# A recurrent attention kernel: one left residual load on ScalarE's queue, main rows stored straight from SBUF, and four steps of the attention one unit later on TensorE

## The chip, the core and the metric

The kernel runs on one core of a Trainium2 chip. The metric is the device time of one execution in microseconds; lower is better. Engines are called by what they do: TensorE (PE in the profile, its weight loads PEld), VectorE (DVE), ScalarE (ACT), GpSimd (POOL) and SyncE (SP, which here only issues DMAs).

## What is computed

The input x (2048 x 1024) is layer-normalised. Two branches read the result and are added to x: a dense GELU block B, and an attention A with 32 heads of 128 that runs over 64 segments of 32 rows, one after the other. Each segment is joined with 8 memory rows, and the first 8 rows of its output are the memory rows of the next segment. That makes A a recurrence:

```python
for s in range(n_seg):                      # 64 segments of 32 rows
    xs = x[:, s * seg_len:(s + 1) * seg_len, :]
    h = concatenate([mem, xs], axis=1)      # 8 + 32 rows
    q = einsum('btd,dhe->bhte', h, Wq)      # k and v alike, from Wk and Wv
    scores = einsum('bhqe,bhke->bhqk', q, k) * scale
    scores = where(mask, scores, -1e9)
    o = einsum('bhqk,bhke->bhqe', softmax(scores), v)
    o = einsum('bhte,hed->btd', o, Wo)
    mem = o[:, :M, :]
    outs.append(o[:, M:, :])
# output: x + outs + gelu(xn @ w1 + b1) @ w2 + b2, xn = layernorm(x)
```

## The kernel before

**Stages.** The layer norm and the dense block come first (lines 292 to 613, about the first 420 us); they leave the transposed rows in DRAM as `hr_d` and `hrL_d` and the residual x + B as `R_n`, which is copied from there into the second halves of `hr_d` and `hrL_d` (columns 256 to 511). Then the loop over the 64 segments runs (`for s in range(NSEG)`). Segment s has `g, i4 = divmod(s, 4)`.

**Main rows and left rows.** Only 24 of a segment's 32 rows (`NX`) must go through the recurrence with the memory rows. The other 8, the left rows, of four segments are put together into groups of 32 and carried through the same weights at fixed places: `left_k`, `left_q`, `left_v` and `left_o` say which passes of a segment take left rows along. With `i4 = 1` the output pass takes them (`left_o`), with `i4 = 0` V's first half, with `i4 = 3` (where groups follow) V's second half.

**Weights.** The 64 units of 128 x 2048 bf16 (512 KB) are K, Q and V in two halves of 8 units and O in 16. 46 units lie in SBUF for good. The other 18 are brought anew for each segment: two are copied by VectorE from PSUM (`kept`, line 241), 16 come by DMA from DRAM copies (`Wc_K`, `Wc_Q`, `Wc_V`, `Wc_O`) through six slots. SyncE issues these loads in the order of use, each when `unit_done` (the unit was multiplied) frees a slot.

**The order within a segment** is written by hand; each engine works its instructions in program order. The passes are K0, Q0, K1, Q1, V0, V1 (`half_pass`) and the output pass over the 16 units of O. A `half_pass` takes a dictionary `at`: what is called after which unit. The attention of a half u is made in three steps between the weight products: `scores(u)` (products into the PSUM bank `mixed`, an exponential on ScalarE into `pr_all`, two minima on VectorE as mask), `sums(u)` (sums over the keys, logarithm and two exponentials on ScalarE, two products on VectorE) and `values(u)` (products with V into accumulator banks, copies by ScalarE and VectorE into `d_oL` for u = 0 and `b_oL` for u = 1). The O units 0 to 7 read `d_oL`, 8 to 15 `b_oL`. There are three accumulator banks.

**Residuals and stores.** After the output pass ScalarE copies the memory part of the accumulator (line 1005), TensorE turns it into the next rows (`put_mem`), and VectorE adds the residual (line 1020): `st["res"]` in `hr_home` for main rows, at `left_o` first `st["resL"]`, which lies in `pr_all` (part of `half_home`), for the second half of the columns. `resL` is loaded on GpSimd's queue after the output pass's second unit (line 1000). The main rows of a segment are loaded by `load_x_rows`, through ScalarE's queue for s < 5 and GpSimd's after that. In the first segments GpSimd's queue also carries the last residual copies (`small`, line 455).

Stores of finished rows go through GpSimd: at `left_o` by way of `outL_d`, with i4 = 0 and 3 as four DMAs straight from SBUF (line 1058), and with i4 = 2 by way of `outM_d`: one store to DRAM on GpSimd's queue (line 1052), and in the next segment's output pass, after its third unit, one copy from DRAM to the output on SyncE's queue (`rows_of_main`, line 1055).

Of the kernel before, what the change touches and what calls it, by code (L numbers as in the profile page):

```python
# [10 lines left out]
BF16 = mybir.dt.bfloat16  # L11
# [6 lines left out]
P = 128  # L18
# [19 lines left out]
NX = 24  # L38
NL = SEG - NX
GRP = 4  # L40
NGRP = NSEG // GRP
# [45 lines left out]
def kernel(  # L87
# [16 lines left out]
    nc = tc.nc  # L104
# [3 lines left out]
    out_flat = out.rearrange("b s d -> (b s) d")  # L108
# [10 lines left out]
    dram = ctx.enter_context(tc.tile_pool(name="dram", bufs=1, space=bass.MemoryType.DRAM))  # L119
# [3 lines left out]
    hrL_d = dram.tile([NGRP + 1, P, 512], BF16, name="hrL_d")  # L123
    R_n = dram.tile([S, DM], BF16, name="R_n")
    outL_d = dram.tile([NGRP, 2 * SEG, DM], BF16, name="outL_d")
    outM_d = dram.tile([NGRP, P, 256], BF16, name="outM_d")


    place = nc.lookup_mloc("DynamicDMAScratchLoc")
# [36 lines left out]
    for j in range(4):  # L166
# [11 lines left out]
        out=m, in_=m, pattern=[[1, NX]], compare_op=ALU.is_ge, fill=0.0, base=0, channel_multiplier=-1,  # L178
    )
    for half in range(2):  # L180
        m = mask_left[0:SEG, :, 8 - 8 * half:16 - 8 * half]
        nc.gpsimd.affine_select(
            out=m, in_=m, pattern=[[-8, GRP], [0, 8]], compare_op=ALU.is_ge, fill=0.0, base=0, channel_multiplier=1,
        )
        nc.gpsimd.affine_select(
            out=m, in_=m, pattern=[[8, GRP], [1 if half else 0, 8]], compare_op=ALU.is_ge, fill=0.0,
# [110 lines left out]
    with tc.tile_pool(name="ma", bufs=2) as ma, tc.tile_pool(name="mps", bufs=6, space=PSUM) as mps:  # L297
# [35 lines left out]
        for j in range(4):  # L333
            nc.sync.dma_start(
                out=o_sb[32 * j + NX:32 * j + 32, 0:8, :],
                in_=mem0[:, 256 * j:256 * j + 256].rearrange("m (h e) -> m h e", h=8),
# [4 lines left out]
        for i in range(14):  # L341
            t = slab(f"w2_{i}")[:, :].rearrange("p (c d) -> p c d", d=DM)
# [146 lines left out]
        for tg in range(4):  # L489
# [14 lines left out]
            for fb in range(FC):  # L504
                ps = mps.tile([P, 512], F32, name="ps")
                for kt in range(KT):
# [9 lines left out]
                    out=xb[:, :], in_=ps[:, :], func=ACT.Identity, bias=b1col[:, fb:fb + 1], scale=1.0  # L516
# [4 lines left out]
                    out=u[:, :], in0=u[:, :], scalar1=0.044715, scalar2=1.0, op0=ALU.mult, op1=ALU.add  # L521
# [94 lines left out]
    with tc.tile_pool(name="late", bufs=1) as late, \  # L616
# [65 lines left out]
        for s in range(NSEG):  # L682
            g, i4 = divmod(s, GRP)
# [10 lines left out]
            left_v = [i4 == 0, first or (i4 == 3 and more)]  # L694
            left_o = i4 == 1 or final
            og, slot = divmod(s + 2, GRP)
# [103 lines left out]
            def scores(u, meanwhile=None):  # L800

                kT, qL_ends = st["kT", u], ends(q_home)
                sA = mixed[:, 0:160].rearrange("p (c q) -> p c q", q=40)
                sB = mixed[:, 160:224].rearrange("p (c q) -> p c q", q=16)
                for c in range(4):
                    for j in range(4):
                        q = slice(32 * j, 32 * j + 32)
                        nc.tensor.matmul(  # L808
                            sA[q, c, :], lhsT=kT[:, 4 * c + j, :], rhs=q_home[:, 4 * c + j, :],
                            start=(c == 0), stop=True, skip_group_check=True, tile_position=(0, 32 * j),  # L810
                        )
                    for j in range(4):
                        q = slice(32 * j, 32 * j + 32)
                        nc.tensor.matmul(  # L814
                            sB[q, c, :].rearrange("p (a b) -> p a b", b=NL), lhsT=kL[u][:, 4 * c + j, :],
                            rhs=qL_ends[:, 4 * c + j, :, :],
                            start=False, stop=True, skip_group_check=True, tile_position=(0, 32 * j),
                        )
                pr = pr_all[:, 0:224]
                nc.scalar.activation(out=pr, in_=mixed[:, 0:224], func=ACT.Exp, scale=INV_SQRT_DH)  # L820
                prA = pr[:, 0:160].rearrange("p (c q) -> p c q", q=40)
                prB = pr[:, 160:224].rearrange("p (c q) -> p c q", q=16)
                if meanwhile is not None:
                    meanwhile()
                for p, m in ((prA[:, :, NL:SEG], mask_order), (prB, mask_left[:, i4, :])):
                    n = m.shape[-1]
                    nc.vector.tensor_tensor(out=p, in0=p, in1=m[:, None, :].to_broadcast([P, 4, n]), op=ALU.min)
                st["pr", u] = prA, prB
# [38 lines left out]
            def values(u, rs):  # L867

                V, (pdA, pdB) = st["V", u], st["pd", u]
                av = {r: new_acc() for r in rs}  # L870
                oV = {r: av[r][:, 0:320].rearrange("p (c b q) -> p c b q", c=4, b=2) for r in rs}
                for c in range(4):
                    for r in rs:
                        q = slice(64 * r, 64 * r + 64)
                        nc.tensor.matmul(  # L875
                            oV[r][:, c, :, :], lhsT=V[q, c * P:(c + 1) * P], rhs=pdA[q, c, :, :],
                            start=(c == 0), stop=False, skip_group_check=True, tile_position=(64 * r, 0),
                        )
                    for r in rs:
                        q = slice(64 * r, 64 * r + 64)  # L880
                        nc.tensor.matmul(
                            oV[r].rearrange("p c b (e q) -> p c b e q", q=NL)[:, c, :, ::4, :],
                            lhsT=VL[u][q, c * P:(c + 1) * P], rhs=pdB[q, c, :, :, :],
                            start=False, stop=True, skip_group_check=True, tile_position=(64 * r, 0),
                        )
                for r in rs:
                    cp = nc.vector.tensor_copy if r else nc.scalar.copy
                    out = outs[u][:, 8 * r:8 * r + 8, NL * slot:NL * slot + 40]
                    cp(out=out.rearrange("p (b c) q -> p c b q", b=2), in_=oV[r])
                    let_go(av[r])  # L890
# [66 lines left out]
            if i4 == 0 and more and not first:  # L957
                load_left_rows(g + 1, nc.scalar)
            at = {0: [lambda: scores(1)], 4: [lambda: sums(1)]}
            if left_v[1]:  # L960
                at.update({1: [lambda: values(0, (0,))], 3: [lambda: values(0, (1,))]})
            else:
                at[1] = [lambda: values(0, (0, 1))]
# [18 lines left out]
            if left_v[1]:  # L982
                at = {4: [lambda: values(1, (0,))], 6: [lambda: values(1, (1,))]}
            else:
                at = {5: [lambda: values(1, (0, 1))]}
            if left_v[1] and not first:
                at[9] = [lambda: left_values(1, psV1L)]
            at.setdefault(0, []).append(load_res)
            if i4 == 3:
                at.setdefault(2, []).append(rows_of_main)  # L990
            psX = new_acc()
            for n, unit in enumerate(O_UNITS):
                t = unit_tile(unit)
                o_product(unit, t, psX)
                unit_done(unit)
                for fn in at.get(n, ()):
                    fn()
                if n == 1 and left_o:
                    st["resL"] = pr_all
                    nc.gpsimd.dma_start(out=st["resL"][:, :], in_=hrL_d[og, :, 256:512])  # L1000
            nw = 2 if left_o else 1
            if not final:
                o_sb = nat_home
# [27 lines left out]
            if final:  # L1031
                engines = [nc.sync, nc.scalar, nc.gpsimd]
                n = 0
                for w, r in enumerate(tiles):
                    for b in range(2):
                        cs = slice(256 * (2 * b + w), 256 * (2 * b + w) + 256)
                        pieces = [(rows, slice(64 * b + m0, 64 * b + m0 + NX))]
                        for sl, row in left_rows:
                            p0 = 64 * b + NL * sl
                            pieces.append((slice(row, row + NL), slice(p0, p0 + NL)))  # L1040
                        for o, i in pieces:
                            engines[n % 3].dma_start(out=out_flat[o, cs], in_=r[i, :])
                            n += 1
            elif left_o:
                pairs = [(out_flat[rows, :], outL_d[og, m0:m0 + NX, :])]
                pairs += [
                    (out_flat[row:row + NL, :], outL_d[og, NL * sl:NL * sl + NL, :]) for sl, row in left_rows
                ]
                for o, r in pairs:
                    small.append(lambda o=o, r=r: nc.gpsimd.dma_start(out=o, in_=r))  # L1050
            elif i4 == 2:
                nc.gpsimd.dma_start(out=outM_d[g, :, :], in_=res[:, :])
                o = out_flat[rows, :].rearrange("t (j c) -> j t c", j=4)
                r = outM_d[g, :, :].rearrange("(j t) c -> j t c", j=4)[:, 0:NX, :]
                rows_of_main = lambda o=o, r=r: nc.sync.dma_start(out=o, in_=r)
            else:
                for j in range(4):
                    nc.gpsimd.dma_start(out=out_flat[rows, 256 * j:256 * j + 256], in_=res[32 * j:32 * j + NX, :])
# [37 lines left out]
```

## Time and profile before

| | |
|---|---|
| median of 4 runs | 1881.68 us (1877.14 to 1893.29) |
| the profiled execution | 1885.86 us, of it 1884.2 us span |
| granted TensorE clock, mean | 0.993 |
| TensorE matmul busy | 1726.1 us (92%) |
| VectorE, ScalarE, GpSimd busy | 902.5, 650.9, 233.7 us |
| weight and other loads on SyncE's queue (q1) | 590.16 MB, 82.9% of 16 DMA engines |
| GpSimd's queue (q0), ScalarE's queue (q10) | 16.71 MB, 2.7%; 2.64 MB, 0.4% |
| chain that ended last | PE 42%, DMA 22%, issue 4%, DVE 4%, ACT 2% |

All figures below the second row are of the profiled execution. Matmuls overlap on TensorE, so its busy share is not a share of its peak. The DMA share is the mean busy share of the 16 DMA engines, by the times of their packets; packets overlap a little, so it can come out slightly above 1. A line number can be that of a helper: L706 is every product of K, Q and V, L903 every product of O, L241 every bit copy.

Of the stores at stake the profile has these groups:

| DMA | queue | count | KB each | median us from issue to landing |
|---|---|---|---|---|
| out_dram<-hr_home, L1058 | GpSimd | 124 | 12 | 5.2 |
| outM_d<-hr_home, L1052 | GpSimd | 16 | 64 | 5.0 |
| out_dram<-outM_d, L1055 | SyncE | 16 | 48 | not recorded |
| half_home<-hrL_d (resL), L1000 | GpSimd | 17 | 64 | 5.2 |

### The profile page before, as it was taken

To read this page: it belongs to the slowest core of one execution; us is meant where nothing else is said; L and a number is where in the kernel's file an instruction comes from. 1 tells how busy PE (TensorE), PEld (TensorE's weight loads), DVE (VectorE), ACT (ScalarE), POOL (GpSimd) and SP (SyncE) were. 2 spreads that over 40 slices of the span, in tenths; PEclk is the share of its full clock that TensorE was granted. 3 is DMA by queue.
4 is the path that set the end of the run, shared out by engine and by line. 5 is a ranking of instruction groups with operands and counts; after the bars stand their busy time and mean duration, and the time that the engine had idled before them with its cause. 6 is when DMAs were issued, how large, how long until landed. Compare 5 with 4: busy or idle time off the path is not lost.

```text
span 1884.2 us, 72814 instructions
## 1 busy us (share of the span) xinstructions
PE 1726.1 (92%) x32228; PEld 935.3 (50%) x32228; DVE 902.5 (48%) x2190; ACT 650.9 (35%) x1384; POOL 233.7 (12%) x464
## 2 busy tenths in 40 slices
PE   7999999998899999898999999898999989999887
PEld 3444444444455555455554555454555454555444
DVE  6657484604354444444444444444444444444443
ACT  6334352502233333333333333333333333333333
POOL 0000000001341111111111010101111111111111
PEclk9999999999999999999999999999999999999999
DMA  9821211499999999999999999999999999999998
GB/s 339 264 55 45 54 48 50 160 358 352 339 400 401 382 391 380 374 373 373 379 381 376 386 385 394 377 371 379 383 386 363 375 369 383 382 389 383 375 363 322
DMA packets 219672, 614.17 MB, mean 326 GB/s; under 512 B 45547, under 2 KB 65435, under 8 KB 219356
## 3 DMA queue, kind: packets, MB, share of 16 engines
q1 hardware_dynamic: 200892, 590.16, 82.9%
q0 software_dynamic: 14368, 16.71, 2.7%
q8 instruction: 252, 4.13, 0.9%
q10 hardware_dynamic: 4096, 2.64, 0.4%
q14 instruction: 64, 0.52, 0.1%
HBM read 595.19 MB, written 30.28 MB: 332 GB/s over the span
## 4 chain that ended last, share of the span: by engine, by line
PE 42%; DMA 22%; issue 4%; DVE 4%; ACT 2%; POOL 0%; DVEq 0%; ACTq 0%; POOLq 0%; SPq 0%
PE acc L706 28%; PE acc L903 9%; DMA u<-Wc_K 9%; DMA u<-Wc_O 5%; DMA outL_d<-half_home 4%; DMA u<-Wc_V 2%; DMA u<-Wc_Q 2%; PE acc L875 2%; ACT mixed L849 1%; PE mixed L808 1%; DVE b_oL L764 1%; DVE pd_main L856 1%; ACT mixed L846 1%; PE mixed L814 0%; DVE u L241 0%
## 5 line engine op out<-in xcount | busy, mean ns | idle before, releaser
L706 PE MATMUL acc<-u,hr_home 128*32 128x512 bf16 x11520 | 788.1, 382 | 42.4 <-issue 14.3
L706 PEld LDWEIGHTS <-hr_home 128*32 128x32 bf16 x12288 | 350.3, 97 | 326.2 <-issue 66.8
L706 PE MATMUL acc<-u,hrL 128*32 128x512 bf16 x2880 | 262.1, 381 | 10.4 <-issue 6.9
L903 PE MATMUL acc<-u,d_oL 128*32 128x256 bf16 (+1 forms) x3552 | 179.5, 290 | 26.1 <-issue 13.0
L507 PE MATMUL ps<-u 128*128 128x512 bf16 x896 | 195.8, 381 | 2.6 <-ACT u L391 2.6
L241 DVE TENSOR_SCALAR u<-kept 128x512 uint32<-128x512 uint32 x254 | 163.4, 685 | 36.5 <-PE acc L903 13.5
L903 PEld LDWEIGHTS <-b_oL 128*32 128x32 bf16 x3569 | 112.1, 99 | 72.3 <-issue 40.6
L556 PE MATMUL ps<-u 128*128 128x512 bf16 x672 | 147.0, 379 | 0.0
L903 PEld LDWEIGHTS <-d_oL 128*32 128x32 bf16 (+1 forms) x3552 | 104.2, 98 | 79.3 <-issue 37.2
L507 PEld LDWEIGHTS <-u 128*128 128x128 bf16 x896 | 88.1, 98 | 109.0 <-issue 4.2
L856 DVE TENSOR_TENSOR pd_main<-half_home,mixed 128x320 bf16<-128x320 bf16 x128 | 62.5, 488 | 155.1 <-ACT mixed L849 152.1
L706 PEld LDWEIGHTS <-hrL 128*32 128x32 bf16 x3072 | 92.2, 96 | 64.5 <-issue 28.0
L903 PE MATMUL acc<-u,b_oL 128*32 128x256 bf16 (+1 forms) x1618 | 107.1, 291 | 17.1 <-DMA u<-Wc_O 8.2
L764 DVE STREAM_TRANSPOSE b_oL<-b_oL 128x512 bf16<-128x512 bf16 x128 | 90.6, 708 | 66.1 <-ACT b_oL L750 66.1
L903 PE MATMUL acc<-W_O,b_oL 128*32 128x256 bf16 (+1 forms) x1776 | 109.7, 290 | 7.3 <-issue 7.3
L750 ACT CAST kT<-acc 128x512 bf16<-128x512 f32 x64 | 37.5, 586 | 217.0 <-PE acc L706 217.0
L263 POOL DMA_DIRECT2D hr_home<-hr_d x58 | 32.3, 556 | 615.9 <-PE acc L706 597.1
L750 ACT CAST b_oL<-acc 128x512 bf16<-128x512 f32 x128 | 75.2, 588 | 91.0 <-PE acc L706 91.0
L556 PEld LDWEIGHTS <-u 128*128 128x128 bf16 x672 | 65.3, 98 | 77.3 <-DVE g_u L523 0.4
L1005 ACT CAST d_oL<-acc 128x256 bf16<-128x256 f32 (+1 forms) x63 | 26.9, 427 | 215.4 <-PE acc L903 215.4
L515 ACT ACTIVATE g_xb<-ps,b1col 128x512 bf16<-128x512 f32 x112 | 76.8, 686 | 60.8 <-PE ps L507 59.6
L849 ACT ACTIVATE mixed<-mixed,small_consts 128x160 f32<-128x160 f32 x256 | 94.2, 368 | 8.4
(124 smaller groups left out, 1943.5 us busy)
## 6 DMA issues: line engine op xcount, KB each, us to landing
u<-Wc_K SPq DMA_DIRECT2D x320, 512.0 KB
u<-Wc_V SPq DMA_DIRECT2D x256, 512.0 KB
u<-Wc_O SPq DMA_DIRECT2D x256, 512.0 KB
u<-Wc_Q SPq DMA_DIRECT2D x128, 512.0 KB
u<-Wc_O SPq DMA_DIRECT2D x64, 320.0 KB
hr_home<-hr_d POOLq DMA_DIRECT2D x58, 128.0 KB, 5.4
u<-in_B_w_dram SPq DMA_DIRECT2D x14, 512.0 KB
u<-in_A_Wq_dram SPq DMA_DIRECT2D x14, 512.0 KB
```

What stands on the lines that cost most here:

```text
L241: nc.vector.tensor_single_scalar(out=out, in_=in_, scalar=0, op=ALU.bitwise_or)
L263: eng.dma_start(out=hr_home[:, 0:n], in_=hr_d[s, :, 0:n])
L507: nc.tensor.matmul(ps[:, :].rearrange("p (s t) -> p s t", t=SEG), lhsT=w1_sb[fb // 14 * 8 + kt][:, (fb % 14) * P:(fb % 14 + 1) * P], rhs=x ...
L515: nc.scalar.activation(out=xb[:, :], in_=ps[:, :], func=ACT.Identity, bias=b1col[:, fb:fb + 1], scale=1.0)
L556: nc.tensor.matmul(ps[:, :], lhsT=gts[fc // 4][:, fc % 4, t * P:(t + 1) * P], rhs=w2_sb[fc // 2][:, fc % 2, cs], start=(fc == 0), stop=(fc ...
L706: nc.tensor.matmul(o, lhsT=lhs[:, i, :], rhs=m, start=(i == seq[0]), stop=(i == seq[-1]), tile_position=(0, 32 * j),)
L750: cp(out=out, in_=ps.rearrange("p (h e) -> p h e", e=32))
L764: nc.vector.transpose(out=home, in_=home)
L849: nc.scalar.activation(out=mixed[:, 160 * b:160 * b + 160], in_=mixed[:, 0:160], func=ACT.Exp, scale=-1.0, bias=off[:, b:b + 1],)
L856: nc.vector.tensor_tensor(out=pdA.rearrange("p c b q -> p b c q"), in0=prA[:, None, :, :].to_broadcast([P, 2, 4, 40]), in1=dd, op=ALU.mult,)
L875: nc.tensor.matmul(oV[r][:, c, :, :], lhsT=V[q, c * P:(c + 1) * P], rhs=pdA[q, c, :, :], start=(c == 0), stop=False, skip_group_check=True ...
L903: nc.tensor.matmul(acc[r:r + n // 8, c:c + wide], lhsT=lhs[:, 4 * (i % 4) + 2 * u + k, :], rhs=w_t[:, c0 + c:c0 + c + wide], start=(unit = ...
```

## The change

Three edits. The load of `resL` after the second O unit goes through ScalarE's queue where s < 5. The stores of the main rows at i4 = 2 take the four DMAs that i4 = 0 and 3 have; the tensor `outM_d`, the store to it and the later copy are gone. In segments whose V passes take no left rows (i4 = 1 and 2, and the last segment, 33 in all) `scores(1)`, `values(0)` and `sums(1)` come after units 1, 2 and 5 of V's second half in place of 0, 1 and 4, and `values(1)` after O unit 6 in place of 5.

```diff
             at = {0: [lambda: scores(1)], 4: [lambda: sums(1)]}
-            if left_v[1]:
+            if not left_v[0] and not left_v[1]:
+                at = {1: [lambda: scores(1)], 2: [lambda: values(0, (0, 1))], 5: [lambda: sums(1)]}
+            elif left_v[1]:
                 at.update({1: [lambda: values(0, (0,))], 3: [lambda: values(0, (1,))]})
             else:
                 at[1] = [lambda: values(0, (0, 1))]
...
             if left_v[1]:
                 at = {4: [lambda: values(1, (0,))], 6: [lambda: values(1, (1,))]}
             else:
-                at = {5: [lambda: values(1, (0, 1))]}
+                at = {5 if left_v[0] else 6: [lambda: values(1, (0, 1))]}
...
             at.setdefault(0, []).append(load_res)
-            if i4 == 3:
-                at.setdefault(2, []).append(rows_of_main)
...
                 if n == 1 and left_o:
                     st["resL"] = pr_all
-                    nc.gpsimd.dma_start(out=st["resL"][:, :], in_=hrL_d[og, :, 256:512])
+                    (nc.scalar if s < 5 else nc.gpsimd).dma_start(
+                        out=st["resL"][:, :], in_=hrL_d[og, :, 256:512]
+                    )
...
-            elif i4 == 2:
-                nc.gpsimd.dma_start(out=outM_d[g, :, :], in_=res[:, :])
-                o = out_flat[rows, :].rearrange("t (j c) -> j t c", j=4)
-                r = outM_d[g, :, :].rearrange("(j t) c -> j t c", j=4)[:, 0:NX, :]
-                rows_of_main = lambda o=o, r=r: nc.sync.dma_start(out=o, in_=r)
             else:
                 for j in range(4):
                     nc.gpsimd.dma_start(out=out_flat[rows, 256 * j:256 * j + 256], in_=res[32 * j:32 * j + NX, :])
```

More of the change, by code (lines that the diff above doesn't have):

```diff
@@ L125 @@
     outL_d = dram.tile([NGRP, 2 * SEG, DM], BF16, name="outL_d")
-    outM_d = dram.tile([NGRP, P, 256], BF16, name="outM_d")
     place = nc.lookup_mloc("DynamicDMAScratchLoc")
```

## The prediction

> **What bounds the kernel now.** I read the page's slices first, then busy time by stretch, then the waits around the three places that the diff touches. The slices:
>
> ```profile
> PE   7999999998899999898999999898999989999887
> ...
> DMA  9821211499999999999999999999999999999998
> ```
>
> From the ninth slice on (377 us, at 47.1 us a slice) both TensorE and the 16 DMA engines show eights and nines. Which of them sets the pace is read from stretches (columns: length; busy us and instructions of PE, PEld, DVE, ACT, POOL; granted clock; DMA share; GB/s):
>
> ```profile
> 476.00:482.00 6.00, 6.00 (x95) 3.09 (x97) 1.79 (x4) 1.01 (x2) 1.66 (x3) 1.00 1.02 393
> 482.00:488.00 6.00, 2.31 (x44) 0.95 (x36) 0.22 (x1) 0.59 (x1) 0.57 (x1) 0.94 0.96 348
> 488.00:494.00 6.00, 4.77 (x48) 1.82 (x52) 3.12 (x7) 0.59 (x1) 2.81 (x6) 0.50 0.40 115
> 494.00:500.00 6.00, 5.80 (x157) 3.20 (x153) 3.06 (x10) 2.87 (x7) 3.13 (x6) 0.99 0.79 258
> 500.00:1850.00 1350.00, 1230.62 (x28483) 700.96 (x28482) 620.65 (x1484) 456.86 (x1055) 201.54 (x382) 0.99 1.00 381
> ```
>
> Over 500 to 1850 us TensorE is idle 119 us of 1350, while the DMA share is 1.00: the stage waits for the weight stream. There a TensorE wait costs time only where it holds back a slot so long that the DMA engines run dry. They do not run flat out: 1850 to 1874 us shows 405 GB/s at a share of 1.03, against 381. At 405 the stage's 514 MB would take 1269 us, so up to 81 us hang on how evenly slots come free. This is why TensorE waits are not worth exactly nothing.
>
> The one hole is at 488 to 500 us, in segments 1 and 2. Its cause (start, length, engine, line, what, idle before and its releaser), first GpSimd, then VectorE, then TensorE:
>
> ```profile
> 478.44 0.55 POOL L455 DMA_DIRECT2D hrL_d<-R_n  x1
> 482.88 0.57 POOL L1000 DMA_DIRECT2D half_home<-hrL_d  x1 [3.89 <-PE acc L706]
> ```
> ```profile
> 488.42 0.42 DVE L1020 TENSOR_TENSOR half_home<-acc,half_home 128x256 bf16<-128x256 f32 x1 [6.21 <-DMA half_home<-hrL_d]
> ```
> ```profile
> 489.23 1.04 PE L706 MATMUL acc<-u,hr_home 128*32 128x512 bf16 x8 [4.92 <-DVE hr_home L1020]
> ```
>
> In segment 1 the left residual is issued at 482.88, behind GpSimd's small copies, and lands 5.4 us later. VectorE's add waits 6.21 us; nothing else on VectorE passes it, and TensorE, which needs the accumulator bank, stands 4.92 us. With no slot freed the stream runs dry, and the clock granted to TensorE is 0.50 until 494.
>
> **Part 1, the left residual on ScalarE's queue.** In the program this touches segment 1 alone: the condition is s < 5, and such loads occur at i4 = 1. ScalarE's two loads of that segment are issued at 473.58 and 474.16, 0.33 us each, and in the planned order the new one follows, ahead of the casts to b_oL (476.56) and of the accumulator (481.01). Its waits are one DMA semaphore and VectorE's; VectorE's last reader of the destination (L860) ends at 473.98, about 474.2 once it is moved by a unit. So I put the issue at 474.6, with 2 us of slack before the next cast. Landing: in segment 0 the second of two such loads was issued at 451.95 and VectorE's add waited for it until 458.92, 7.0 us; 474.6 + 7.0 = 481.6. The add could start at 482.22. A third load in the queue may be 1 us later than that. The stall falls from 6.2 us to between 0 and 1.
>
> What it is worth is the DMA time that was lost, since the stage behind is DMA-bound: (1.00 - 0.40) x 6 + (1.00 - 0.79) x 6 = 3.6 + 1.3 = 4.9 us, as much as TensorE's 4.92. I take -4.9, with bounds -6.2 (VectorE's whole wait) and 0 (the load late again). Next late is VectorE's wait for the main load, at most about 1 us (0.99 in segment 0).
>
> A rule weighs against it. The Trainium skill, "Trainium Kernel Development and Optimization", section Key Constraints, says that queues of SP, ACT and POOL feed the same 16 DMA engines and that issuing from several saves the issue time alone; by that the move would save L1000's 0.57 us. The row shows an in-order backlog on GpSimd, which the rule leaves out, so I go by the row.
>
> **Part 2, main rows straight from SBUF.** At each of 16 segments with i4 = 2, a 64 KB store to outM_d on GpSimd's queue (0.56 us of issue) and, in the next segment's output pass, a 48 KB copy DRAM to DRAM on SP's queue (0.65 us of issue) go. Four stores of 12 KB from GpSimd come, as i4 = 0 and 3 have them. DMA time of the two kinds on GpSimd's queue, from 14 us stretches that hold one of each (first 1226 to 1240, then 1248 to 1262):
>
> ```profile
> q0 software_dynamic: 32, 0.07, 1.4%
> ```
> ```profile
> q0 software_dynamic: 128, 0.05, 1.3%
> ```
>
> That is 0.014 x 14 = 0.20 us removed and 0.013 x 14 = 0.18 us added, about even. The copy of 48 KB lies within the weight queue, where the page gives no price of its own. Bounds: 0, if it fills gaps, and 0.65, if SP's hold, in which no weight load can be issued, counts in full. Its bytes at 381 GB/s are 49152 / 381e3 = 0.13 us; I take that, as the nearest row is the stage's own rate. Sum per group -0.02 - 0.13 = -0.15, x 16 = -2.4 us. The ends: +2.9, if what goes had filled gaps and the new 0.18 us counts 16 times, and 16 x (0.02 + 0.65) = -10.7. GpSimd's issue grows from 0.56 to 4 x 0.52 = 2.1 us, hidden: its next work, L263, is issued 14.67 us after (1227.00, 1241.67). In segment 2 three more issues stand before the small copies, but GpSimd comes out of part 1 some 6 us earlier. SP's next weight loads, queued behind the copy, get its 0.65 us.
>
> The rule against it: "DMA: Bandwidth & Descriptors", section Anatomy of one DMA — SWDGE (gpsimd) path, fits 2.0 us fixed plus bytes / 436e3 per DMA; taken one after another, four of 12 KB (8.1 us) against the two removed (2.15 + 2.11) would add 3.9 us a group, 62 us in all, an estimate from that page. The trace lets them overlap: four issued within 2.09 us (1248.89), each landing after 5.2 us in the median, nobody waiting. I keep the sum above.
>
> **Part 3, one unit later.** The order by engine shows that TensorE alone is rearranged: in 33 segments (i4 = 1 and 2, and the last) four products of V's second half, a unit, pass in front of scores(1), another in front of values(0) and of sums(1), and one O unit in front of values(1). No instruction of ScalarE or VectorE changes place. A unit takes 6.48 / 30 = 0.216 us (120 products in 6.48 on the chain), an O unit at left rows 0.43.
>
> Gain: scores(1) waits for the transpose of b_oL:
>
> ```profile
> L808 PE MATMUL mixed<-b_oL,d_oL 128*32 128x40 bf16 x1024 | 26.6, 182 | 16.3 <-DVE b_oL L764 10.8 <-issue 5.5
> ```
>
> Over 64 segments; half is 8.2 us, and one unit of cover covers at most 33 x 0.216 = 7.1. Loss: after values(1) the copies to b_oL need 0.49 us (L889 on VectorE) and some 0.07 to start; before, two O units cover this (0.43 or 0.86), afterwards one (0.22 or 0.43). That exposes about 0.21 us each time, 33 x 0.21 = 6.9 us. So TensorE gets 7.1 and gives 6.9, both in a stage where it isn't the bound. I take 0, with ends -7.1 and +6.9. Slots: the first streamed unit of V1 comes free one score block earlier (about 0.3 us), which can only feed the stream sooner.
>
> **Sum.** -4.9 - 2.4 + 0 = -7.3 us against the profiled execution's 1885.86 us (span 1884.2): 1878.6. That execution stands 0.22% above the median of the runs, 1881.68, so the forecast is 1881.7 - 7.3 = 1874 us, 0.4% less.
>
> **Rivals.**
> - *Faster, 1863 us or less.* The stream's 81 us of unevenness shrinks: scores' cover pays in full (-7.1), its exposure falls where DMA waits hide it, and the copy's 0.65 us hold of SP counts each time (-10.4): -4.9 - 7.1 - 10.4 = -22.4, 1859. For it: output passes at i4 = 3, where the copy sits, are poor in GB/s (1240 to 1247: 355). Against: the share is 1.00.
> - *Slower.* values(1) with one unit left before b_oL is read: the whole copy shows, not the difference, 0.49 + 0.07 each time, and scores' gain lies under the stream's waits: 33 x 0.56 = 18.5, less 7.3, gives +11 us, 1893. It decides from 7.3 / 33 = 0.22 us a segment on. Against: today's row for this wait is 3.6 us over 15 times (weight loads of L903 released by L889).
> - *No change, about 1881.* The load on ScalarE's queue is as late as GpSimd's, or blocks the cast to b_oL behind it, so that the hole stays. For it: the load's wait is in order on an engine that TensorE needs. Against: the 2 us of slack. Then only part 2 is left.
>
> **Numbers.** Forecast 0.62 (1867 to 1881), faster rival 0.14 (half of it beyond 1%), slower 0.12, no change 0.12. 1% of 1881.7 is 18.8 us, about what a measurement can tell from no change. The range 1862 to 1886 takes in the forecast with both ends of part 3, the no-change case and the near half of the other two. Faster by over 1% 0.08, slower by over 1% 0.05, within 0.87.
>
> **What would show it.** Part 1: VectorE's wait for half_home<-hrL_d in segment 1 is gone, the DMA share of the matching stretch is 0.95 or more, and no clock of 0.50 stands there. Part 2: GpSimd's out_dram<-hr_home stores go from 124 to 188, no group outM_d, nobody waits for the new ones, and the GB/s of 500 to 1850 stays at 381 or rises. Part 3: L808's idle on d_oL falls by some 7 us, weight loads of L903 on b_oL wait for L889 by 5 to 9 us more, and the DMA share stays at 1.00. I am wrong if the share falls below 0.98, or if TensorE's idle in that stretch changes by over 10 us and the span with it.

## The result, and the profile after

The changed kernel takes 1876.59 us (median of 43 runs, 1864.32 to 1883.79) against 1882.48 us (62 runs): a ratio of 0.9964, 95% interval 0.9951 to 0.9976, that is 6.8 us less by the ratio (4.5 to 9.2) and 5.9 us between the two medians. The forecast was 7.3 us less. The profiled execution after took 1875.87 us, of it 1874.2 us span.

The same stretches as before, around the hole and over the steady stage (columns as in the prediction):

```profile
482.00:488.00 6.00, 6.00 (x144) 3.22 (x140) 3.13 (x7) 1.76 (x3) 2.18 (x4) 1.00 1.03 392
488.00:494.00 6.00, 4.32 (x124) 2.08 (x116) 3.42 (x9) 2.63 (x7) 2.04 (x4) 1.00 1.02 402
494.00:500.00 6.00, 4.61 (x143) 3.17 (x144) 3.41 (x9) 2.49 (x7) 1.72 (x4) 1.00 1.01 376
500.00:1840.00 1340.00, 1225.38 (x28287) 699.93 (x28283) 617.67 (x1474) 452.74 (x1046) 223.78 (x427) 1.00 1.00 381
```

The shares of 0.40 and 0.79 are now 1.02 and 1.01, and the clock of 0.50 is gone. What made it so, in the timeline of ScalarE and of VectorE:

```profile
472.34 0.33 ACTq L969 DMA_DIRECT2D hr_home<-hr_d  x1
473.08 0.33 ACTq L999 DMA_DIRECT2D half_home<-hrL_d  x1
475.60 0.43 ACT L888 CAST b_oL<-acc 128x320 bf16<-128x320 f32 x1 [3.10 <-PE acc L880]
```
```profile
481.45 0.42 DVE L1021 TENSOR_TENSOR half_home<-acc,half_home 128x256 bf16<-128x256 f32 x1 [0.48 <-DMA half_home<-hrL_d]
```

The load is issued 2.5 us ahead of the next cast and holds nothing up; VectorE waits 0.48 us where it waited 6.21. The groups that part 3 touches, first two of the kernel before, then three of the changed one (there L902, L888, L807 and L763 are what L903, L889, L808 and L764 were):

```profile
L903 PEld LDWEIGHTS <-b_oL 128*32 128x32 bf16 x3008 | 78.8, 97 | 46.8 <-issue 40.6 <-ACT b_oL L889 3.6
L903 PEld LDWEIGHTS <-b_oL 128*64 128x64 bf16 x561 | 33.2, 110 | 25.5
```

```profile
L902 PEld LDWEIGHTS <-b_oL 128*32 128x32 bf16 x3008 | 77.6, 96 | 51.7 <-issue 43.7 <-ACT b_oL L888 4.6
L902 PEld LDWEIGHTS <-b_oL 128*64 128x64 bf16 x561 | 31.9, 110 | 29.2 <-ACT b_oL L888 7.1
L807 PE MATMUL mixed<-b_oL,d_oL 128*32 128x40 bf16 x1024 | 25.8, 182 | 6.6 <-DVE b_oL L763 5.0 <-issue 1.5
```

scores(1) (L807) waits 6.6 us in all where it waited 16.3: 5.8 us of the gain is the wait for the transpose of b_oL (10.8 to 5.0), the other 4 is "issue", idle time for which the profile names no cause. The weight loads of the first reader of b_oL (L902) wait 4.6 + 7.1 us for its copies (L888) where the wait was 3.6 and nothing. So products get some 10 us, and weight loads give some 8; the two are not the same thing, as a later run shows.

Part 2 shows in the page's groups (line, engine and operation, then busy us, mean ns, and the idle time before with what ended it) and in its DMA queues (packets, MB, share of 16 engines; q1 carries SyncE's, q0 GpSimd's):

```profile
L1054 POOL DMA_DIRECT2D out_dram<-hr_home x188 | 96.4, 513 | 316.7 <-DVE hr_home L1021 304.6
```
```profile
q1 hardware_dynamic: 199292, 589.38, 83.1%
q0 software_dynamic: 15872, 16.39, 2.6%
```

188 stores stand there; 304.6 of the 316.7 us of idle time before them ended with VectorE's add that makes the rows. q1 has 0.78 MB less than before (16 copies of 48 KB); q0's share is 2.6% where it was 2.7%. No bytes of weight are saved by any part; what changes is how early they come.

### The profile page after: what moved, and what is told of

Read it like the earlier page. It is cut to its first block, busy times and chain, and to the rows that moved or that the text cites. A ratio compares the mean times of both kernels' runs of the same rounds, so it can differ in the third digit from the quotient of the medians.

```text
span 1874.2 us, 72891 instructions
## 1 busy us (share of the span) xinstructions
PE 1724.9 (92%) x32228; PEld 937.9 (50%) x32228; DVE 903.7 (48%) x2190; ACT 649.9 (35%) x1384; POOL 256.8 (14%) x511
## 3 DMA queue, kind: packets, MB, share of 16 engines
q1 hardware_dynamic: 199292, 589.38, 83.1%
## 4 chain that ended last, share of the span: by engine, by line
PE 42%; DMA 19%; issue 3%; DVE 3%; ACT 2%; POOL 0%; DVEq 0%; ACTq 0%; POOLq 0%
PE acc L705 29%; PE acc L902 9%; DMA u<-Wc_K 7%; DMA u<-Wc_O 7%; DMA outL_d<-half_home 3%; DMA u<-Wc_V 2%; PE acc L874 1%; PE mixed L807 1%; ACT mixed L848 1%; DVE b_oL L763 1%; DVE pd_main L855 1%; PE mixed L813 0%; DVE u L240 0%; DMA u<-Wc_Q 0%; PE mixed L834 0%
## 5 line engine op out<-in xcount | busy, mean ns | idle before, releaser
L902 PE MATMUL acc<-u,d_oL 128*32 128x256 bf16 (+1 forms) x3552 | 177.0, 290 | 23.6 <-DMA u<-Wc_O 14.6
L902 PEld LDWEIGHTS <-b_oL 128*32 128x32 bf16 x3569 | 109.5, 98 | 80.9 <-issue 43.7
L902 PEld LDWEIGHTS <-d_oL 128*32 128x32 bf16 (+1 forms) x3552 | 105.7, 98 | 74.2 <-issue 35.7
L1054 POOL DMA_DIRECT2D out_dram<-hr_home x188 | 96.4, 513 | 316.7 <-DVE hr_home L1021 304.6
L902 PE MATMUL acc<-u,b_oL 128*32 128x256 bf16 (+1 forms) x1618 | 107.2, 290 | 20.9 <-DMA u<-Wc_O 10.7
L763 DVE STREAM_TRANSPOSE b_oL<-b_oL 128x512 bf16<-128x512 bf16 x128 | 90.6, 708 | 64.8 <-ACT b_oL L749 64.8
L902 PE MATMUL acc<-W_O,b_oL 128*32 128x256 bf16 (+1 forms) x1776 | 109.7, 290 | 7.2 <-issue 7.2
```

Source lines behind the costliest of these rows:

```text
L763: nc.vector.transpose(out=home, in_=home)
L902: nc.tensor.matmul(acc[r:r + n // 8, c:c + wide], lhsT=lhs[:, 4 * (i % 4) + 2 * u + k, :], rhs=w_t[:, c0 + c:c0 + c + wide], start=(unit = ...
```

## The experiments

All ratios are against the kernel before on the same chip. The theory at the start: the stream of weights sets the pace, so only DMA time lost or saved counts.

**Each part alone.** The kernel before with one of the three edits, and the changed kernel with part 1 undone (`(nc.scalar if s < 5 else nc.gpsimd)` against `nc.gpsimd`).

> The kernel before with part 1 alone (the left residual through ScalarE's queue for s < 5). Theory (the weight stream sets the pace, and only DMA time lost or saved counts): -4.9 us against the kernel before, ratio 0.9974; in the trace VectorE's wait for half_home<-hrL_d in segment 1 is under 1 us and the DMA share from 488 to 500 us is 0.95 or more. Rival (the gain came from the stores or from the order on TensorE): the hole is filled but made up elsewhere, ratio 0.999 to 1.001.

> The kernel before with part 2 alone (main rows of i4 = 2 straight from SBUF). Theory: -2.4 us, ratio 0.9987, the hole at 488 us stays. Rival (SyncE's hold of 0.65 us counts each time): -10.7 us, ratio 0.994. Rival (the copy only filled gaps): 1.000 or +2.9 us.

> The kernel before with part 3 alone (scores, values and sums one unit later). Theory: TensorE gains about 7 us at scores(1) and gives as much at b_oL, off the bound: ratio 1.000, within 0.002. Rival (the better cover of scores(1) counts): -7 us, ratio 0.996. Rival (the lost cover of the copies to b_oL counts): +7 us, ratio 1.004.

> The changed kernel with part 1 undone (parts 2 and 3 stay). Theory: +4.9 us against the changed kernel, so -2 us against the kernel before, ratio 0.999; VectorE waits some 6 us for half_home<-hrL_d again and the granted clock is 0.50 for some 6 us. Rival: ratio as for the whole change, 0.9964.

| kernel | median us | ratio | 95% interval |
|---|---|---|---|
| part 1 alone | 1876.04 | 0.9970 | 0.9944 to 0.9997 |
| part 2 alone | 1879.30 | 0.9995 | 0.9974 to 1.0016 |
| part 3 alone | 1884.94 | 1.0013 | 0.9990 to 1.0037 |
| parts 2 and 3 | 1879.44 | 1.0001 | 0.9981 to 1.0022 |

Part 1 alone gives 5.6 us (0.6 to 10.5 by its interval) where 4.9 was expected; without it the change gives nothing that can be told from zero. Part 2's 0.9 us and part 3's +2.4 us lie within their intervals. In the profile of part 1 alone VectorE does not wait for the left residual at all, and the hole is filled:

```profile
488.00:494.00 6.00, 3.89 (x80) 1.83 (x80) 2.10 (x8) 2.09 (x6) 1.92 (x4) 1.00 0.99 384
494.00:500.00 6.00, 5.69 (x188) 3.68 (x181) 4.14 (x10) 3.22 (x8) 3.24 (x7) 1.00 0.98 319
```

With parts 2 and 3 it is back:

```profile
482.00:488.00 6.00, 0.00 (x0) 0.00 (x0) 0.00 (x0) 0.21 (x1) 0.57 (x1) 0.84 0.66 235
488.00:494.00 6.00, 5.13 (x60) 2.13 (x64) 3.39 (x7) 0.58 (x1) 3.15 (x6) 0.59 0.36 107
494.00:500.00 6.00, 6.00 (x184) 3.46 (x172) 3.54 (x10) 3.31 (x8) 2.78 (x6) 1.00 0.90 311
```

Its lost DMA time is (0.34 + 0.64 + 0.10) x 6 = 6.5 us, and the kernel lies 0.0037, 7 us, above the changed one. So part 1 is shown, with its mechanism. The same three stretches lose 5.1 us in the kernel before and 7.0 us with part 3 alone (shares 0.98, 0.28 and 0.57): with part 3 and without part 1, VectorE waits 8.6 us for the late load instead of 6.2. Most of part 3's +2.4 us can be this deeper hole, which part 1 takes away.

**Main rows by way of DRAM everywhere, and not stored at all.**

```diff
-                for j in range(4):
-                    nc.gpsimd.dma_start(out=out_flat[rows, 256 * j:256 * j + 256], in_=res[32 * j:32 * j + NX, :])
+                nc.gpsimd.dma_start(out=outM_d[s, :, :], in_=res[:, :])
...
+                rows_of_main = lambda o=o, r=r: nc.sync.dma_start(out=o, in_=r)
```

> The changed kernel, but with the main rows of i4 = 0, 2 and 3 (47 segments, where the kernel before did it in 16) stored to DRAM and copied from there on SyncE's queue in the next segment's output pass. Theory (bytes and packets count, 0.15 us a segment): +7 us against the changed kernel, 1.000 against the kernel before. Rival (SyncE's hold of 0.65 us counts each time): 47 x 0.67 = +31 us, ratio 1.013. Rival (the copy fills gaps): as the changed kernel, 0.9964.

> The changed kernel without any store of the main rows of i4 = 2 (these rows of the output are left out). Theory (DMA time counts even where nobody waits): 16 x 0.18 = -2.9 us against the changed kernel, 0.995. Rival (stores nobody waits for are free): 0.9964.

By DRAM everywhere: 1881.67 us, 0.9993 (0.9970 to 1.0017). That is 0.0029 above the change, 5.5 us for 47 segments; the theory's 7 us fits, though the intervals leave room from near 0 to 11 us; the 31 us of a SyncE hold that counts in full is excluded. Without the stores: 1873.85 us, 0.9964 (0.9939 to 0.9988), the change's own ratio; the 2.9 us expected are below what this resolves.

**The order on TensorE: two units later, and values(1) put back.**

```diff
-                at = {1: [lambda: scores(1)], 2: [lambda: values(0, (0, 1))], 5: [lambda: sums(1)]}
+                at = {2: [lambda: scores(1)], 3: [lambda: values(0, (0, 1))], 6: [lambda: sums(1)]}
...
-                at = {5 if left_v[0] else 6: [lambda: values(1, (0, 1))]}
+                at = {5 if left_v[0] else 7: [lambda: values(1, (0, 1))]}
```

The second kernel has the changed kernel's `at` for V and `at = {5: [lambda: values(1, (0, 1))]}` for O.

> The changed kernel with part 3 done twice: scores(1), values(0), sums(1) after units 2, 3 and 6, values(1) after O unit 7, so that no unit lies between values(1) and the first reader of b_oL. TensorE should wait 33 x 0.21 = 7 us more there. Theory (TensorE is not the bound): as the changed kernel, 0.9964, within 0.002. Rival (TensorE's order counts): +7 us, 1.000.

> The changed kernel with values(1) back after O unit 5: the gain of part 3 without its loss. Theory: as the changed kernel, 0.9964, within 0.002, though the weight loads of L903 wait some 7 us less for the copies to b_oL. Rival (TensorE's order counts): -7 us against the changed kernel, 0.993.

Two units later: 1888.01 us, 1.0027 (1.0004 to 1.0050), 0.0063 or 12 us above the change (7 to 17 by the intervals). Here the theory fell: the same loads are issued, and only TensorE's order differs. TensorE's waits in this kernel, 500 to 1840 us (waits in total, times, longest), first its weight loads, then its products:

```profile
PEld L902 <- ACT b_oL L888: 22.4, 44, 0.7
```
```profile
PE acc L902 <- ACT b_oL L888: 15.6, 31, 0.5
```

In the changed kernel the same two rows are

```profile
PEld L902 <- ACT b_oL L888: 10.5, 31, 0.5
```
```profile
PE acc L902 <- ACT b_oL L888: 0.4, 2, 0.2
```

With one unit of cover only the weight loads waited, and the products hardly; with none the products stand 0.5 us each time. values(1) back after unit 5: 1871.51 us, 0.9939 (0.9916 to 0.9961), and the wait of the weight loads falls from 10.5 to

```profile
PEld L902 <- ACT b_oL L888: 3.4, 14, 0.2
```

**The price of DMA time and of TensorE time, apart.** One kernel gets an extra DMA, the other extra products:

```diff
...
+                if n == 2:
+                    nc.sync.dma_start(out=extra_d[s, :, :], in_=W_v["K"][0:64, 0, 0:2048])
```
```diff
...
                     product(w, i, t, hT, ps, range(KT))
+                    if (w, u) == ("V", 1) and i in (0, 2, 4, 5):
+                        product(w, i, t, hT, ps, ())
```

> The changed kernel with one more DMA per segment on SyncE's queue after the third O unit: 256 KB copied DRAM to DRAM, read by nobody. Theory (the weight stream is the bound): 64 x 0.262 MB at 381 GB/s = 64 x 0.69 = +44 us, ratio 1.020 against the kernel before. Rival (TensorE is the bound and the DMA engines have room): at most +5 us, 0.999.

> The changed kernel with four units of V's second half multiplied twice in every segment (the second product is added into the same sums, so V's second half is another one): 64 x 4 x 0.216 = 55 us more on TensorE. Theory (TensorE has 1.9 us of idle per segment under the weight stream): 0 to +15 us, ratio 0.996 to 1.005. Rival (TensorE is the bound): +55 us, ratio 1.026.

More bytes: 1902.34 us, 1.0096 (1.0049 to 1.0144); more products: 1908.57 us, 1.0137 (1.0110 to 1.0164). Over the change's 0.9964 that is 25 us for 44 us of copies and 33 us for 55 us of products: each counts for about 0.6 of itself (by the intervals 0.4 to 0.8 for the copies, 0.5 to 0.7 for the products), and neither theory nor rival holds alone. One thing is not told apart: an extra copy also holds SyncE's queue for 0.50 us, 32 us in all, and a part of the 25 us may be that. By the all-by-DRAM kernel it is a small part, as 47 copies, which held the queue 0.65 us each in the kernel before, cost 5.5 us with their bytes. The steady stage, first with more bytes, then with more products:

```profile
500.00:1840.00 1340.00, 1210.33 (x27896) 703.26 (x27898) 609.50 (x1453) 445.00 (x1028) 216.74 (x414) 0.99 1.00 386
```
```profile
500.00:1840.00 1340.00, 1236.55 (x28619) 707.71 (x28623) 606.89 (x1441) 441.49 (x1018) 217.33 (x415) 1.00 0.99 372
```

With more products the DMA share reads 0.99 still, though the engines move 372 GB/s where they moved 381. So a share near 1.00 does not show that the stream is saturated; how far the GB/s lie below the 405 of the best stretch is the better mark here.

**The change beside values(1) put back, on one chip.**

> The changed kernel itself, on the same chip as the next run: 0.9964 against the kernel before, within 0.002.

> The changed kernel with values(1) back after O unit 5, beside the changed kernel on one chip. New theory (TensorE time and DMA time each count for about 0.6 of themselves, from +33 us for 55 us of products and +25 us for 44 us of copies): 7 us less wait for the copies to b_oL give -4 us, ratio 0.002 under that of the changed kernel. First theory (only the weight stream counts): the same ratio as the changed kernel.

The change: 1876.07 us, 0.9955 (0.9931 to 0.9980). Put back: 1873.61 us, 0.9941 (0.9914 to 0.9967). The difference is 0.0014 here and was 0.0025 between the earlier runs, both the new theory's way; the intervals overlap each time. The version with values(1) back beats the kernel before; that it beats the changed kernel is likely and not shown. The wait that it saves is one of weight loads, while the products waited 0.4 us in the changed kernel, so a gain of nothing stays possible.

The profile of the version put back shows what is late next. In that execution a hole stood at the old place again, with part 1 in (two stretches, then ScalarE, then GpSimd):

```profile
488.00:494.00 6.00, 0.83 (x24) 0.32 (x16) 0.93 (x4) 0.36 (x1) 0.13 (x1) 0.72 0.72 278
494.00:500.00 6.00, 6.00 (x128) 2.65 (x120) 3.34 (x9) 2.80 (x7) 4.47 (x9) 0.71 0.57 177
```
```profile
492.65 0.36 ACT L819 ACTIVATE half_home<-mixed 128x224 bf16<-128x224 f32 x1 [5.45 <-DMA outL_d<-half_home]
```
```profile
486.10 0.56 POOL L1026 DMA_DIRECT2D outL_d<-half_home  x1 [2.95 <-DMA u<-Wc_V]
```

The store of the finished left rows stands on GpSimd's queue as the left residual did. ScalarE may not overwrite `half_home` before it has landed, and TensorE stood 5.17 us behind. The two stretches lost (0.28 + 0.43) x 6 = 4.3 us of DMA time, yet this execution took 1868.17 us, the third fastest of 11 (1864.90 to 1877.47): a single execution's time does not show a hole of this size. In eight profiles of other executions with part 1 in, ScalarE's wait at this place is 0.7 to 2.5 us and there is no such hole. So part 1 cured one late DMA of that queue, and another is only just in time.

## Why the prediction was right

*Part 1* held by its mechanism and in size: 4.9 us expected, 5.6 measured alone. The timing came out by two errors that cancel: the load was issued at 473.08, 1.5 us earlier than put, and took 8.4 us until the add began (481.45, put at 481.6), not 7.0. The slack ahead of the cast was 2.5 us where 2 was put. The weighing of the rule on queues held: more than the 0.57 us of issue time was saved. What held the load on GpSimd is less clear than the prediction has it. Its row names TensorE (3.89 us); with part 1 undone the same gap (4.35 us) has no releaser, and with part 3 alone (3.61 us) it is put down to ScalarE. VectorE's last read of the destination had ended at 473.98. So the wait belongs to GpSimd's queue, and its cause is open. "Next late" was put at about 1 us for the main load; it is the store of left rows, up to 5.45 us.

*Part 2* was put at 2.4 us; 0.9 was measured, with an interval of some 4 us to either side, and the kernel with all main rows by DRAM gives 5.5 / 47 = 0.12 us a segment, near the 0.15 of the sum. Part 2 alone excludes the gain of 10.7 us, and the 62 us of loss from the page's fit per DMA; that estimate also priced SyncE's copy by a fit for GpSimd's path. The stores went from 124 to 188. The only recorded wait for the landing of one is GpSimd's own, ahead of the last segment's residual load: 5.7 us, where the old store cost it 4.9.

*Part 3* was put at zero for two reasons: gain and loss cancel, and TensorE isn't the bound. The first is right in the sizes (the wait at b_oL grew by 8 us, 5 to 9 were expected; scores(1) gained 10, 5.8 of it from the transpose, where 7 was expected), but the gain is products' wait and the loss is weight loads' wait, and that a microsecond of one pays for one of the other is not shown. The second is the step that failed: TensorE's time counts for about 0.6 of itself in that stage. That the zero fits is partly luck; a step with a plain gain or loss, as the one two units later, would have been put at zero wrongly. The prediction had the warning in its text, the 81 us between 381 and 405 GB/s, and read it as "not exactly nothing". 10 us gained and 8 given, at 0.6 each, leave about 1 us, and 10 gained with nothing given would be 6 us; part 3 alone, at +2.4 us with some 4 us to either side and its deeper hole, speaks against the second and does not settle it.

*The sum* is closer than its terms: the parts measured alone give -5.6 - 0.9 + 2.4 = -4.1 us, and each is known to 4 or 5 us only. The change as a whole, -6.8, is known to 2.4 us to either side, far better than the 18.8 us that the prediction thought a measurement could tell.

The slower rival's price for a fully shown copy, 33 x 0.56 = 18.5 us, is what the two-units-later kernel shows in the products' wait (15.6 us), one unit further on than the rival had it.

## What to carry to other kernels

When two engines are both near full, price a microsecond of each by adding a known amount of work to one at a time; a share of 1.00 on one of them doesn't make the other's time free. Moving a step by one unit changes the cover on both of its sides: count what waits before it and what reads its result, and keep the side that pays. A single late load on a backed-up queue in the first segments can be worth more than edits to all of the others; look there for the one wait that is longer than the rest, and then for the next DMA on the same queue.

## What was not expected of the hardware

The DMA share stayed at 0.99 to 1.00 while the moved bytes fell from 381 to 372 GB/s with more products. Over the whole run the weight queue's packets took 82.4% of 1909.8 us for the same 589.38 MB that took 83.1% of 1874.2 us, 1% more. So a part of the fall shows as longer packet times and not as gaps. And GpSimd's queue waited up to 3 to 5 us at a time between small copies in segments 1 and 2 with no releaser in the profile (3.08 us ahead of the last copies of segment 1 in the kernel before, 4.54 in the changed one, 4.80 with part 1 undone, 5.27 with the hole above). What GpSimd waits for there was not tried.
